# Decay attention, MLP and gated convolution on one core: two sums of each half unit as adding DMAs, a third place for z, and ks by transposes

## The chip, the cores and the metric

The kernel runs on one core of one Trainium2 chip. The metric is the time of one execution on the device in microseconds (us); lower is better. The engines: TensorE (PE, with its weight loads as PEld), VectorE (DVE), ScalarE (ACT), GpSimd (POOL) and SyncE (SP), which starts the DMAs. "Granted clock" is the share of TensorE's full speed that it was given.

## What is computed

Three blocks follow one another, for 4 batches, 8 heads, 768 positions and a head size of 48 (8 x 48 = 384 columns). All data are float32; the weights come as float64 words and are taken apart on the chip.

```python
mag = np.sqrt(a_re * a_re + a_im * a_im)
scale = np.minimum(mag, 0.999) / (mag + 1e-06)
for t in range(S):                      # attention with a complex decay
    S_re, S_im = ar * S_re - ai * S_im + k_t (x) v_t, ar * S_im + ai * S_re
    y[:, :, t] = q_t . S_re
u = x + (x^T @ U @ V)^T                 # mixes all positions of a batch
x = u + relu(u @ w_ch1) @ w_ch2
gate = sigmoid(conv5(x))
out = (gate * (x @ w_val)) @ w_out
```

## The kernel before, in words

`chunked_path` writes the program as a list of operations (class `Program`): each has an engine, an estimated cost, and its dependences. A list scheduler (`lay`, `order`) then sets the order on each engine by urgency plus a bias from the table `URGE`, whose keys are a stage and an engine ("a12S": batch 1, third unit, SP; "m00V": batch 0, first MLP half, DVE; "w3A": weights, fourth group, ACT). On the chip each engine, SP's and POOL's queues among them, runs its operations in that order; only semaphores hold it. `T` makes a tile in a pool; a pool with `bufs` places per tag makes a new tile wait until the oldest one's readers are through.

A batch's attention (`attention`, called by `attend`) runs in three *units* of 256 positions, named by batch and first position (0, 256, 512). The 128 partitions hold 8 heads x 16 groups of 16 positions. Each unit has these stages:

- `z` (pool `p2`, two places) receives `a_re` and `a_im`. In `xa` the decay is normalised, in two halves ("groups"), and `z` becomes the running product over 8 positions (`s1`, `s2`).
- The products are combined across the groups (`qd`, `psT`, `un`, `tot`, `cx`, `psC`), and give the factors `fs`. The result carried to the next unit is `ng`.
- The correction, once for each half, in the loop over `groups`: three products with `fs` put one part into `xc` (as `y2`) and the other into `z`; DVE adds `y2` to `z` (128x768); ACT squares it; DVE adds real and imaginary squares (128x384); ACT takes a logarithm and an exponential; DVE makes `qh` and the scaled `z` with `q` and `k`.
- `z` is stored to a DRAM tile `kd`, and `z` and `qh` are transposed on PE (`pst`) and copied by ACT into `kT` and `qT`.
- For each of the unit's two chunks of 128 positions: `ks`, the same keys with positions on the partitions, is loaded from `kd` (not for the last chunk of a batch); PE makes the scores (`pss`, masked by DVE into `mt`), the state update (`pkv`, added into `st`) and the output (`py`, copied to `yt`). `yt` goes to DRAM (`yd`), and `pxu` collects `xu`, the product with `U`, over the batch.

`moe(b)` then works in two halves of 384 positions: `pu` (with `xuh`, made from `xu`), `m3u`, twelve steps of `ph`, `hp` and `px`, `m3x`, the gate `g`, `pv`, `m3g`, `po`, and the store of `ob`. Each fp32 product is three matmuls of split operands (`mm3`), so DVE and ACT split every operand. `moe(0)` needs the `xu` of all three units of batch 0. Attention of batch b+1 is spread among the matmuls of `moe(b)`. `load_weights` loads 30 raw tiles of 384 KB and converts each: a shift and two merges on DVE (`wt`), two checks and a copy on ACT (`ab`, `w`), a subtraction on DVE (`w`). `w1s` and `w2s` serve `ph` and `px`, `wvs` and `wos` serve `pv` and `po`. The conversions are free to stand anywhere in the order; they run among batch 0's attention.

In the rows all tensor operations have the line of a helper: L551 `tt` (DVE), L567 `stt`, L579 `tsc`, L589 `act`, L600 and L612 matmuls, L621 `transpose`, L631 `dma`. So an operation is named by its tiles.

Of the kernel before, what the change touches and what calls it, by code (L numbers as in the profile page):

```python
# [499 lines left out]
def chunked_path(ctx, tc, outer, q, k, v, a_re, a_im, moe_U, moe_V, w1, w2, w_val, conv_w, w_out, out):  # L500
# [219 lines left out]
    def load_weights():  # L720
# [7 lines left out]
        raw = []  # L728
        for i, (_, _, src, kk, c) in enumerate(todo):
            st = T("wts", [128, PW, 2], I32, f"w{i}", f"raw{i}")  # L730
            sv = src.bitcast(I32).rearrange("(k p) f -> k p f", p=128)[kk]
            dma(st.rearrange("p n w -> p (n w)"), sv[:, 2 * PW * c : 2 * PW * (c + 1)])
            raw.append(st)
        for i, (to, key, *_) in enumerate(todo):
            g.kind = f"w{i // 6}"
            x = T("p3", [128, PW], F32, "g", f"wt{i}")
            single(x, raw[i])
            to[key] = T("wts", [128, 2, PW], F32R, f"w{i}", f"w{i}")
            act(to[key][:, 0], x)
            sub("V", to[key][:, 1], x, f32(to[key][:, 0]))  # L740
# [12 lines left out]
    def attention(b, u0, R):  # L753
# [129 lines left out]
        kd = T("dram", [128, R * 2 * D], F32, "kd", "kd" + n)  # L883
        kdw = kd.rearrange("(h k) f -> k h f", k=16)
# [3 lines left out]
        dma(qk[:, 0], rows(q))  # L888
        dma(qk[:, 1], rows(k))
        qk = qk.rearrange("p c (j d) -> p c j d", d=D)  # L890
        x = T("p1", [128, 16 * 3 * D], F32, "xc", "xc" + n)[:, : R * 3 * D].rearrange("p (j c d) -> p j c d", c=3, d=D)
# [310 lines left out]
```

## Time and profile before

| | us |
|---|---|
| Median of 3 runs (lowest, highest) | 761.53 (759.87, 761.7) |
| The profiled execution's own time | 758.62 |
| Its span | 756.9 |
| PE busy | 620.4 (82%) |
| PEld busy | 567.6 (75%) |
| DVE busy | 622.6 (82%) |
| ACT busy | 445.0 (59%) |
| POOL busy | 2.7 (0%) |
| DMA queue of SP | 67.86 MB, 33.3% of 16 engines' time |

The shares are means over stages with different limits. In the profile's strip of 40 slices, PE is nearly idle in the first three and near full from the tenth on, and DVE is at 9 tenths from the second slice through most of the program. A row of the profile names an operation as out<-in with its shape; an "idle before" time names what ended the engine's wait. In the chain of waits each piece was released by the one before it. The granted clock is 0.94 on average.

### The profile page before, as it was taken

How to read it: one execution, taken by the hardware profiler on the slowest of the kernel's cores; microseconds unless marked ns; L12 is line 12 of the kernel's file. 1: busy time of each engine (PE TensorE's matmuls, PEld its weight loads, DVE VectorE, ACT ScalarE, POOL GpSimd, SP SyncE). 2: the span in 40 equal slices, each digit the busy share in tenths (PEclk: the TensorE clock that was granted, in tenths of full speed). 3: DMA queues.
4: the chain of work that ended last, by engine and by line, in shares of the span. 5: the costliest groups of instructions: out<-in, count | busy, mean ns of one | idle time of the engine just before them, and what ended most of it. 6: DMA issues, size and time to landing. Idle time of an engine off the chain costs nothing.

```text
span 756.9 us, 12129 instructions
## 1 busy us (share of the span) xinstructions
PE 620.4 (82%) x4314; PEld 567.6 (75%) x4314; DVE 622.6 (82%) x1545; ACT 445.0 (59%) x1100; POOL 2.7 (0%) x31
## 2 busy tenths in 40 slices
PE   0003927768997999989999899999999999999994
PEld 0002816556996999869988799889899998899984
DVE  5999999999989989999599899897898875516261
ACT  7899935656458654774478437843774545414253
POOL 1000000000000000000000000000000000000000
PEclk9999558697999999999999999999999999999997
DMA  6984506460052640540515503413142231100000
GB/s 130 320 310 123 128 21 157 120 159 26 1 146 64 162 108 4 147 105 2 144 45 160 133 1 103 108 43 104 43 127 74 64 94 42 43 1 1 1 32 36
DMA packets 80740, 68.71 MB, mean 91 GB/s; under 512 B 52000, under 2 KB 67360, under 8 KB 80672
## 3 DMA queue, kind: packets, MB, share of 16 engines
q1 hardware_dynamic: 80672, 67.86, 33.3%
q8 instruction: 36, 0.59, 0.3%
q14 instruction: 32, 0.26, 0.1%
HBM read 48.97 MB, written 18.87 MB: 90 GB/s over the span
## 4 chain that ended last, share of the span: by engine, by line
PE 53%; DVE 25%; ACT 10%; DMA 8%; issue 2%; SPq 1%; ACTq 0%; DVEq 0%
PE ph L600 17%; PE px L600 16%; DVE z L551 4%; DVE xc L551 4%; PE pss L600 3%; PE py L612 3%; PE pv L600 3%; PE po L600 3%; ACT xa L589 3%; DVE g L567 3%; DMA z<-in_a_im_dram 3%; DMA kd<-z 2%; DVE s L551 2%; PE pkv L612 2%; DMA ks<-kd 2%
## 5 line engine op out<-in xcount | busy, mean ns | idle before, releaser
L600 PE MATMUL ph<-m3u,w 128*128 128x384 f32 x864 | 209.8, 351 | 3.0 <-ACT m3u L589 2.5
L600 PE MATMUL px<-hp,w 128*128 128x384 f32 x864 | 206.2, 345 | 0.4 <-DVE xt L551 0.4
L600 PEld LDWEIGHTS ph<-m3u,w 128*128 128x128 f32 x864 | 156.4, 193 | 9.2 <-ACT m3u L589 4.1
L600 PEld LDWEIGHTS px<-hp,w 128*128 128x128 f32 x864 | 152.4, 188 | 3.7 <-issue 1.9
L589 ACT ACTIVATE hp<-ph 128x384 fp32r<-128x384 f32 x96 | 46.7, 489 | 105.3 <-PE ph L600 97.3
L567 DVE SCALAR_TENSOR_TENSOR hp<-ph,hp 128x384 fp32r<-128x384 f32 x96 | 52.8, 553 | 59.0 <-ACT hp L589 58.7
L600 PE MATMUL pss<-qT,kT 96*128 96x128 f32 x384 | 56.5, 291 | 6.5 <-ACT qT L589 6.5
L600 PEld LDWEIGHTS pss<-qT,kT 96*128 96x128 f32 x384 | 52.2, 203 | 9.4 <-ACT qT L589 8.0
L551 DVE TENSOR_TENSOR s<-xa,z 128x192 f32<-128x192 f32 x168 | 54.6, 351 | 0.8 <-ACT z L589 0.2
L567 DVE SCALAR_TENSOR_TENSOR g<-xt,cw,g 128x384 f32<-128x384 f32 x96 | 53.0, 609 | 0.0
L600 PE MATMUL pv<-m3x,w 128*128 128x384 f32 x216 | 47.0, 358 | 4.8 <-DVE m3x L551 3.9
L621 PE MATMUL pst<-eye_r,xc 128*96 128x128 f32 x192 | 32.7, 292 | 21.2 <-ACT xc L589 18.6
L600 PE MATMUL po<-w,m3g 128*128 128x384 f32 x216 | 47.2, 352 | 3.2 <-ACT m3g L589 2.2
L621 PE MATMUL psT<-eye_r,qd 128*96 128x128 f32 x24 | 5.8, 325 | 47.0 <-ACT qd L589 47.0
L600 PEld LDWEIGHTS pv<-m3x,w 128*128 128x128 f32 x216 | 38.3, 195 | 7.5 <-DVE m3x L551 5.2
L589 ACT ACTIVATE xa<-xa,cb 128x384 f32<-128x384 f32 x72 | 41.8, 610 | 3.5 <-DVE xa L567 2.0
L600 PEld LDWEIGHTS po<-w,m3g 128*128 128x128 f32 x216 | 36.5, 188 | 8.3 <-ACT m3g L589 2.9
L621 PEld LDWEIGHTS pst<-eye_r,xc 128*96 128x96 f32 x192 | 23.7, 135 | 24.4 <-ACT xc L589 18.8
L612 PEld LDWEIGHTS pkv<-vt,ks 128*96 128x96 f32 x320 | 32.4, 178 | 9.3 <-DMA ks<-kd 3.7
L612 PE MATMUL py<-mt,vt 128*64 128x128 f32 x384 | 39.0, 292 | 0.1
L621 PEld LDWEIGHTS psT<-eye_r,qd 128*96 128x96 f32 x24 | 3.0, 147 | 47.9 <-ACT qd L589 47.5
L612 PE MATMUL pkv<-vt,ks 128*96 128x48 f32 x320 | 32.9, 260 | 7.1 <-DMA ks<-kd 7.1
(150 smaller groups left out, 1162.9 us busy)
## 6 DMA issues: line engine op xcount, KB each, us to landing
raw<-in_moe_w_ch_dram SPq DMA_DIRECT2D x24, 384.0 KB, 8.0
kd<-z SPq DMA_DIRECT2D x24, 384.0 KB, 3.8
ks<-kd SPq DMA_DIRECT2D x20, 384.0 KB, 4.2
z<-in_a_re_dram SPq DMA_DIRECT2D x12, 384.0 KB, 4.7
z<-in_a_im_dram SPq DMA_DIRECT2D x12, 384.0 KB, 5.6
qk<-in_k_dram SPq DMA_DIRECT2D x12, 384.0 KB, 4.2
qk<-in_q_dram SPq DMA_DIRECT2D x12, 384.0 KB, 5.2
vt<-in_v_dram SPq DMA_DIRECT2D x24, 192.0 KB, 3.0
```

The costliest lines, as they stand in the source:

```text
L551: e, cost, lambda: engines[e].tensor_tensor(out=real(o), in0=real(a), in1=real(b), op=op), views(a, b), [o]
L567: lambda: nc.vector.scalar_tensor_tensor(out=real(o), in0=real(a), scalar=real(s), in1=real(b), op0=o0, op1=o1),
L589: return nc.scalar.activation(real(o), real(a), func, scale=real(scale), **kw)
L600: "P", cost, lambda: nc.tensor.matmul(real(o), real(lhsT), real(rhs), start=start, stop=stop),
L612: r = nc.tensor.matmul(ro[idx], real(lhsT), real(rhs), start=start, stop=stop)
L621: op = g.add("P", cost, lambda: nc.tensor.transpose(real(o), real(a), real(idn)), views(a, idn), [o])
```

## The change

Five things are changed:

- In batches 1 to 3 the two sums of each half (`z` plus `y2`, and the two squares) are DMAs issued by POOL that add into their target in SBUF (`dma_add`, called by `more`). In batch 0 both stay on DVE.
- In batch 0 the second unit's `z` has a place of its own, `wo2`, beside the two of `p2`. After it the place holds the raw tiles 28 and 29 (of `w_out`) together, and then their split; both are converted after the second of them.
- In batch 0 no `kd` is written. `ks` is made on PE by four transposes of `kT` at a time (`psk`), copied by ACT.
- `xc` is laid out so that `y2` and the squares lie contiguously.
- The scheduler's costs for some DMAs and all of `URGE` are other numbers, so the whole order is another.

```diff
     def dma(o, a, slow=1.0):
...
-        cost = max(475.0, time)
+        cost = max(475.0, x.shape[0] * x.free / 80.0)
...
+    def dma_add(o, x):
+        time = x.shape[0] * x.free / 67.5
+        return g.add(
+            "G", 560.0, lambda: nc.gpsimd.dma_start(real(o), real(x), accum_op=ALU.add), views(o, x), [o], lat=1500.0 + 1.6 * time
+        )
...
+    BY_DMA = (1,2,3,)
...
+        two = T("wts", [128, 2, PW, 2], I32, "wo2", "raw_wo2")
...
-            st = T("wts", [128, PW, 2], I32, f"w{i}", f"raw{i}")
+            st = two[:, i - 28] if 28 <= i < 30 else T("wts", [128, PW, 2], I32, f"w{i}", f"raw{i}")
...
+        def more(o, x):
+
+            if b in BY_DMA:
+                dma_add(o, x)
+            else:
+                add("V", o, o, x)
...
-        z = T("p2", [128, 16 * 2 * D], F32, "z", "z" + n)[:, : R * 2 * D]
+        z_at = ("wts", "wo2") if b == 0 and u0 == UT else ("p2", "z")
+        z = T(z_at[0], [128, 16 * 2 * D], F32, z_at[1], "z" + n)[:, : R * 2 * D]
...
-            add("V", z, z, y2)
-            act(y2, z, AF.Square)
-            add("V", x2, x0, x1)
-            act(x0, x2, AF.Ln, bias=cb[:, 6:7])
+            more(z.rearrange("p j c d -> p (j c d)"), y2)
+            act(sq, z, AF.Square)
+            nn = sq[:, :, 0]
+            more(y2[:, : nj * D], y2[:, nj * D :])
+            act(x0, nn, AF.Ln, bias=cb[:, 6:7])
...
-            dma(kdw[:, :, j0 * P2 : j1 * P2], z.rearrange("p j c d -> p (j c d)"))
+            if b:
+                dma(kdw[:, :, j0 * P2 : j1 * P2], z.rearrange("p j c d -> p (j c d)"), 2.2)
...
-                dma(ks, kdv[c * kr : (c + 1) * kr].rearrange("k j h e -> (k j) h e"), 1.4)
+                if b:
+                    dma(ks, kdv[c * kr : (c + 1) * kr].rearrange("k j h e -> (k j) h e"), 1.4)
+                else:
+                    for h0 in range(0, H, 4):
+                        psk = T(many[0], [C, 4, P2], F32, many[1], "psk" + nc_)
+                        for i in range(4):
+                            transpose(psk[:, i], kTv[:, h0 + i, cs], ident[:P2, :P2])
+                        act(ks[:, h0 : h0 + 4], psk)
```

Where the order moves, first on DVE just before the first MLP half of batch 0. In the names, a number behind a tile's name is the unit's first position or a buffer; `xa_256` here is batch 1's second unit. Before:

```order
L579 TENSOR_SCALAR wt_1603<-raw_598 128x384
L567 SCALAR_TENSOR_TENSOR wt_1590<-raw_701,wt_1590 128x384
L551 TENSOR_TENSOR xu_993<-xu_993,pxu_512_1584 128x96
L551 TENSOR_TENSOR w_1566<-wt_1452,w_1566 128x384
L567 SCALAR_TENSOR_TENSOR wt_1603<-raw_598,wt_1603 128x384
L579 TENSOR_SCALAR wt_1618<-raw_772 128x384
L567 SCALAR_TENSOR_TENSOR wt_1590<-raw_701,wt_1590 128x384
L551 TENSOR_TENSOR xa_256_1576<-xa_256_1576 128x8x48 x2
L551 TENSOR_TENSOR xl_1639<-xu_993,xh_1627 128x96
L567 SCALAR_TENSOR_TENSOR xa_256_1576<-xa_256_1576 128x8x48
L579 TENSOR_SCALAR xuh_1629<-xl_1639 32x96 x8
```

Of the change, up to the same `xuh`:

```order
L553 TENSOR_TENSOR w_1610<-wt_1491,w_1610 128x384
L569 SCALAR_TENSOR_TENSOR xa_256_1531<-xa_256_1531 128x8x48 x2
L553 TENSOR_TENSOR xa_256_1531<-z_256_1447,xa_256_1531 128x8x96
L553 TENSOR_TENSOR xu_1165<-xu_1165,pxu_512_1631 128x96
L553 TENSOR_TENSOR xa_256_1531<-z_256_1447,xa_256_1531 128x8x96
L553 TENSOR_TENSOR xl_1660<-xu_1165,xh_1655 128x96
L553 TENSOR_TENSOR s_1_0_1663<-un_0_1617 96x128
L581 TENSOR_SCALAR xuh_1657<-xl_1660 32x96 x8
```

All thirty tiles' shifts stand ahead of `xuh` before, and 24 of the change; between the last `xu` and `xuh` no weight is left, and batch 1's second unit is further on.

PE, at the third unit of batch 0, first chunk. Before, where `ks` is loaded by a DMA:

```order
L621 MATMUL pst_512_1422<-eye_r,xc_512_1251 96x128 x4
L600 MATMUL pss_512_0_1439<-qT_512_1354,kT_512_1375 128x128 x4
L600 MATMUL pss_512_0_1450<-qT_512_1354,kT_512_1375 128x128 x4
L612 MATMUL py_512_0_1464<-qT_512_1354,st_128 64x128 x2
...
L600 MATMUL pss_512_1_1492<-qT_512_1354,kT_512_1375 128x128 x3
L612 MATMUL pkv_512_0_1501<-vt_122,ks_512_0_1454 96x48 x8
```

Of the change:

```order
L623 MATMUL pst_512_1455<-eye_r,xc_512_1353 96x128 x4
L623 MATMUL psk_512_0_1465<-eye_r,kT_512_1410 128x96 x4
L623 MATMUL psk_512_0_1475<-eye_r,kT_512_1410 128x96 x4
L602 MATMUL pss_512_0_1488<-qT_512_1396,kT_512_1410 128x128 x4
L602 MATMUL pss_512_0_1498<-qT_512_1396,kT_512_1410 128x128 x4
L614 MATMUL pkv_512_0_1505<-vt_122,ks_512_0_1478 96x48 x8
```

`pkv` has moved from behind the chunk's `py` and the next chunk's first scores to right behind its own scores, and its `ks` comes from two groups of transposes.

ACT in the first unit of batch 1, where the adds begin (`xc_0` is that unit's, its squares read the `z_0` that a DMA has added to, and the rows with `cb` are the logarithms behind the second add). Of the change:

```order
L591 ACTIVATE xc_0_1875<-z_0_816 128x8x2x48
L591 ACTIVATE tot_256_1980<-ng_0_1858 96x2x8
L591 ACTIVATE w_1982<-wt_1791 128x384
L591 ACTIVATE hp_0_1993<-ph_0_1925 128x384
L591 ACTIVATE xc_0_1875<-z_0_816 128x8x2x48
L591 ACTIVATE hp_0_2020<-ph_0_1954 128x384
L591 ACTIVATE un_256_1961<-un_256_1961 96x96 x2
L591 ACTIVATE xc_0_1875<-xc_0_1875,cb 128x384
L591 ACTIVATE xc_0_1875<-xc_0_1875 128x384
L591 ACTIVATE w_2047<-wt_1977 128x384
L591 ACTIVATE hp_0_2057<-ph_0_2015 128x384
L591 ACTIVATE xc_0_1875<-xc_0_1875,cb 128x384
```

The `hp` copies that free `ph` for PE stand between the squares and logarithms that wait for the adds.

## Rows read from the trace of the kernel before

**Rows 1.** Busy time by stretch: us, length, busy (x instructions) by engine, clock, DMA.
```profile
0.00:176.50 176.50, 73.32 (x537) 58.74 (x537) 165.99 (x442) 131.85 (x372) 2.34 (x28) 0.82 0.58 160
176.50:745.00 568.50, 545.44 (x3768) 507.63 (x3769) 456.51 (x1103) 309.50 (x714) 0.33 (x3) 0.99 0.27 70
745.00:756.90 11.90, 1.67 (x11) 1.27 (x9) 0.14 (x1) 3.66 (x16) 0.00 (x0) 0.73 0.16 56
```

**Rows 2.** PE's timeline at the first ph: start us, us, operation, idle before.
```profile
176.55 1.80 PE L600 MATMUL ph<-m3u,w 128*128 128x384 f32 x4 [0.81 <-ACT m3u L589]
```

**Rows 3.** Waits of PE, 176 to 757 us: us in total, times, longest us.
```profile
PE pv L600 <- DVE m3x L551: 3.9, 4, 1.6
...
PE pkv L612 <- DMA ks<-kd: 3.1, 3, 2.4
PE ph L600 <- ACT m3u L589: 2.5, 4, 0.8
```

**Rows 4.** Busy time in two passages between MLP halves, columns as in group 1.
```profile
230.00:250.00 20.00, 15.64 (x129) 13.22 (x128) 19.94 (x39) 16.64 (x34) 0.11 (x1) 1.00 0.21 53
330.00:350.00 20.00, 16.73 (x84) 13.84 (x81) 19.67 (x64) 10.17 (x34) 0.00 (x0) 0.91 0.23 66
```

**Rows 5.** Chain of waits, 149 to 162 us: start us, us, what.
```profile
149.59 0.88 DVE z L551
...
150.49 5.03 DMA kd<-z
...
155.53 3.93 DMA ks<-kd
...
159.50 1.56 PE pkv L612 x16
```

**Rows 6.** Timeline of ACT and PE, 145 to 154 us, third unit of batch 0.
```profile
147.19 0.49 ACT L589 ACTIVATE xo<-pxt 128x384 f32<-128x384 f32 x1 [1.71 <-PE pxt L621]
...
150.56 1.05 PE L621 MATMUL pst<-eye_r,z 128*96 128x128 f32 x8 [0.20 <-ACT qT L589]
...
152.49 0.59 ACT L589 ACTIVATE kT<-pst 96x512 f32<-96x512 f32 x1
```

**Rows 7.** Timeline of DVE, 81 to 89 us.
```profile
82.40 0.55 DVE L567 SCALAR_TENSOR_TENSOR wt<-raw,wt 128x384 int32<-128x384 int32 x1
...
83.77 1.02 DVE L551 TENSOR_TENSOR xa<-xa 128x384 f32<-128x384 f32 x2
```

**Rows 8.** Groups of DVE by form: count, busy us, mean ns, idle before.
```profile
L551 DVE TENSOR_TENSOR mt<-pss,cmask 128x512 f32<-128x512 f32 x48 | 32.4, 683 | 2.1 <-PE pss L600 1.8
...
L551 DVE TENSOR_TENSOR xc<-xc 128x384 f32<-128x384 f32 x48 | 26.0, 549 | 0.1
...
L551 DVE TENSOR_TENSOR z<-z,xc 128x768 f32<-128x768 f32 x24 | 22.6, 949 | 0.1
...
L579 DVE TENSOR_SCALAR wt<-raw 128x384 int32<-128x384 int32 x30 | 10.4, 352 | 0.0
```

**Rows 9.** DMA issues: operation, count, KB each, median us to landing.
```profile
kd<-z SPq DMA_DIRECT2D x24, 384.0 KB, 3.8
...
z<-in_a_re_dram SPq DMA_DIRECT2D x12, 384.0 KB, 4.7
z<-in_a_im_dram SPq DMA_DIRECT2D x12, 384.0 KB, 5.6
...
xt<-yd SPq DMA_DIRECT2D x24, 192.0 KB, 2.6
out_dram<-ob SPq DMA_DIRECT2D x24, 192.0 KB, 1.9
```

**Rows 10.** Groups of ACT by form: square, logarithm, exponential of the correction.
```profile
L589 ACT ACTIVATE xc<-z 128x768 f32<-128x768 f32 x24 | 20.2, 843 | 10.4 <-DVE z L551 10.2
...
L589 ACT ACTIVATE xc<-xc,cb 128x384 f32<-128x384 f32 x24 | 14.5, 611 | 7.7 <-DVE xc L551 7.7
...
L589 ACT ACTIVATE xc<-xc 128x384 f32<-128x384 f32 x24 | 12.2, 518 | 0.4
```

More of the change, by code (lines that the diff above doesn't have):

```diff
@@ L737, in load_weights @@
             single(x, raw[i])
-            to[key] = T("wts", [128, 2, PW], F32R, f"w{i}", f"w{i}")
-            act(to[key][:, 0], x)
-            sub("V", to[key][:, 1], x, f32(to[key][:, 0]))
+            done = [(i, to, key, x)]
+            if i == 28:
+                late = done
+                continue
+            if i == 29:
+                two = T("wts", [128, 2, 2, PW], F32R, "wo2", "wo2")
+                done = late + done
+            for j, to, key, x in done:
+                to[key] = two[:, j - 28] if i == 29 else T("wts", [128, 2, PW], F32R, f"w{j}", f"w{j}")
+                act(to[key][:, 0], x)
+                sub("V", to[key][:, 1], x, f32(to[key][:, 0]))
     xts, xus, yds, state, carry = {}, {}, {}, {}, {}
@@ L770, in attention @@
         a3 = T("p1", [128, 16 * 3 * D], F32, "xa", "xa" + n)[:, : R * 3 * D].rearrange("p (j c d) -> p j c d", c=3, d=D)
-        z = T("p2", [128, 16 * 2 * D], F32, "z", "z" + n)[:, : R * 2 * D]
-        dma(z[:, : R * D], rows(a_re))
-        dma(z[:, R * D :], rows(a_im))
+        z_at = ("wts", "wo2") if b == 0 and u0 == UT else ("p2", "z")
+        z = T(z_at[0], [128, 16 * 2 * D], F32, z_at[1], "z" + n)[:, : R * 2 * D]
+        dma(z[:, : R * D], rows(a_re), 1.6)
+        dma(z[:, R * D :], rows(a_im), 1.6)
         ab = z.rearrange("p (c j d) -> p j c d", c=2, d=D)
@@ L881, in attention @@
             act(fs_[:, 1, 0], fs_[:, 1, 2], scale=-1.0)
-        kd = T("dram", [128, R * 2 * D], F32, "kd", "kd" + n)
-        kdw = kd.rearrange("(h k) f -> k h f", k=16)
+        if b:
+            kd = T("dram", [128, R * 2 * D], F32, "kd", "kd" + n)
+            kdw = kd.rearrange("(h k) f -> k h f", k=16)
+            kdv = kd.rearrange("(h k) (j e) -> k j h e", k=16, j=R)
         qT = T("p1", [P2, 128 * 16], F32, "qT", "qT" + n)[:, : 128 * R].rearrange("p (h k j) -> p h k j", h=H, j=R)
@@ L887, in attention @@
         qk = T("p1", [128, 2, 16 * D], F32, "qk", "qk" + n)[:, :, : R * D]
-        dma(qk[:, 0], rows(q))
-        dma(qk[:, 1], rows(k))
+        dma(qk[:, 0], rows(q), 1.5)
+        dma(qk[:, 1], rows(k), 1.5)
         qk = qk.rearrange("p c (j d) -> p c j d", d=D)
-        x = T("p1", [128, 16 * 3 * D], F32, "xc", "xc" + n)[:, : R * 3 * D].rearrange("p (j c d) -> p j c d", c=3, d=D)
-        x0, x1, x2 = x[:, :, 0, :], x[:, :, 1, :], x[:, :, 2, :]
-        y2 = x[:, :, 0:2, :]
+        x = T("p1", [128, 16 * 3 * D], F32, "xc", "xc" + n)
         zr, xr = z, x
@@ L896, in attention @@
             b0, b1, nj = j0 // RB, j1 // RB, j1 - j0
-            z, x, zb = zr[:, j0:j1], xr[:, j0:j1], zv[:, b0:b1]
-            x0, x1, x2 = x[:, :, 0, :], x[:, :, 1, :], x[:, :, 2, :]
-            y2 = x[:, :, 0:2, :]
+            z, x, zb = zr[:, j0:j1], xr[:, j0 * 3 * D : j1 * 3 * D], zv[:, b0:b1]
+            y2, x0 = x[:, : 2 * nj * D], x[:, 2 * nj * D :].rearrange("p (j d) -> p j d", d=D)
+            sq = y2.rearrange("p (c j d) -> p j c d", c=2, d=D)
+            qh = y2.rearrange("p (j c d) -> p j c d", c=2, d=D)
             ms = [128, nj, 2, D]
@@ L902, in attention @@
             bs = [128, b1 - b0, RB, 2, D]
-            yv = y2.rearrange("p (b j) c d -> p b j c d", b=b1 - b0)
+            yv = qh.rearrange("p (b j) c d -> p b j c d", b=b1 - b0)
             mul("V", yv, fs_[:, b0:b1, 0:2].unsqueeze(2).to_broadcast(bs), zb[:, :, :, 1:2, :].to_broadcast(bs))
@@ L906, in attention @@
             mul("V", zb[:, :, :, 0, :], fs_[:, b0:b1, 1:2].to_broadcast(hf), zb[:, :, :, 0, :])
-            add("V", z, z, y2)
-            act(y2, z, AF.Square)
-            add("V", x2, x0, x1)
-            act(x0, x2, AF.Ln, bias=cb[:, 6:7])
+            more(z.rearrange("p j c d -> p (j c d)"), y2)
[3 more added lines that the diff above has]
+            act(x0, nn, AF.Ln, bias=cb[:, 6:7])
             act(x0, x0, AF.Exp, scale=-1.0)
-            mul("V", x2, x2, x0)
+            mul("V", nn, nn, x0)
             mul("V", x0, qk[:, 1, j0:j1], x0)
-            stt(x0, x2, 2.0, x0, ALU.subtract, ALU.mult)
-            qh = x[:, :, 1:3, :]
+            stt(x0, nn, 2.0, x0, ALU.subtract, ALU.mult)
             mul("V", qh, qk[:, 0, j0:j1].unsqueeze(2).to_broadcast(ms), z)
             mul("V", z, x0.unsqueeze(2).to_broadcast(ms), z)
-            dma(kdw[:, :, j0 * P2 : j1 * P2], z.rearrange("p j c d -> p (j c d)"))
+            if b:
+                dma(kdw[:, :, j0 * P2 : j1 * P2], z.rearrange("p j c d -> p (j c d)"), 2.2)
             for src, dst in ((z, kT), (qh, qT)):
@@ L926, in attention @@
                     act(to, pst.rearrange("p j (k h) -> p k h j", h=H))
-        kdv = kd.rearrange("(h k) (j e) -> k j h e", k=16, j=R)
         qTv = qT.rearrange("p h k j -> p h (k j)")
@@ L942, in attention @@
                 kr = C // R
-                dma(ks, kdv[c * kr : (c + 1) * kr].rearrange("k j h e -> (k j) h e"), 1.4)
+                if b:
+                    dma(ks, kdv[c * kr : (c + 1) * kr].rearrange("k j h e -> (k j) h e"), 1.4)
[5 more added lines that the diff above has]
+                        act(ks[:, h0 : h0 + 4], psk)
             st = state.get(b)
```

34 rows, old and new, of the table URGE are left out of this document.

## The prediction

> **What bounds the kernel now.** I read three stretches first [rows 1]. Up to 176.5 us TensorE (PE) works 73.3 us and VectorE (DVE) 166.0. From 176.5 to 745 us PE works 545.4 of 568.5, DVE 456.5. The last 12 us are the last store and the flag. The border is the first `ph` of batch 0, at 176.55 us [rows 2]: the MLP of a batch needs `xu` of its whole sequence, so all of batch 0's attention lies before it. The kernel is thus DVE's queue and batch 0's chain up to 176.5, and PE's own work after it. After the border only 568.5 - 545.4 = 23.1 us are open, in small waits of PE, for `m3x`, `m3u` and `ks` among others [rows 3], bunched where one half of the MLP ends and the next begins: in 230 to 250 us PE works 15.6 of 20 and DVE 19.9, in 330 to 350 PE 16.7 and DVE 19.7 [rows 4]. So time comes off in three ways: an earlier first `ph`, shorter passages from half to half, or a stall that PE is spared.
>
> **ks by transposes (batch 0).** Six `kd` stores and five `ks` loads go. In the chain of batch 0's third unit the last `z` product ends at 150.47 us, `kd` takes 5.03 us, `ks` 3.93, and `pkv` starts at 159.50 [rows 5]. In the new order PE runs the two groups of `psk` right behind the unit's `pst`. Their parts: the eight transposes of `z` behind the last product took 1.05 us and ended at 151.61; the last `kT` copy, two groups behind, ended at 153.08; eight more transposes at 1.05 give 154.13; two copies out of PSUM at 0.49 each (the row of `xo`, the same 128x384) give 155.1 [rows 6]. That is 159.5 - 155.1 = **4.4 us** earlier. PE issues 40 more transposes (5 chunks x 1.05 = 5.3 us) and ScalarE (ACT) 10 more copies (4.9 us), where PE is busy 73 of 176.5 us and ACT 131.9 [rows 1]: besides the two copies on the chain, nothing. Were ACT full there, all 4.9 us would come back.
>
> **DVE's queue before the first `ph`.** By the order, before the first `m3u` subtraction DVE now runs 6 fewer `wt` shifts, 9 fewer `wt` merges and 4 fewer `w` subtractions, but 2 more products of 768 columns, 1 more step of 384 and 2 small ones of batch 1. A step of 384 lasts 0.55 us and two of them 1.02, so neighbours overlap by 0.08 [rows 7]; start to start a shift takes 0.35 - 0.08 = 0.27 us, a step of 384 takes 0.47, one of 768 takes 0.87 [rows 8]. So 6 x 0.27 + 13 x 0.47 = 7.7 us less and 2 x 0.87 + 0.47 + 0.3 = 2.5 more: 5.2 us less. The third place for `z` makes this possible: the `xa` and `z` work of units 256 and 512 moves forward, before and among unit 0's corrections, and fills DVE in place of weights. Queue (5.2) and chain (4.4) must both shrink; I take the smaller, **-4.4 us**, which needs both parts. The weights left out come later, among the first half's `ph`; PE needs `wvs` and `wos` only at its end, so I cost that at nothing. The two raw tiles that wait for the third `z` serve `po`, the half's last step: nothing, unless DVE fills up there.
>
> **Adds by DMA (batches 1 to 3).** DVE loses 18 sums of 768 columns and 18 of 384 (3 batches x 3 units x 2 halves; [rows 8] count 24 of the first kind with batch 0's): 18 x (0.87 + 0.47) = 24.1 us of the 456.5. DVE is not what PE waits for most of that time, so only the passages count. From the first `m3x` of a half to the next half's first `hp`, six times, DVE has 332 rows before and 343 in the new order; each at its shape's mean less the overlap of 0.08, they take 140.2 us and 137.1: 14 fewer steps of 384, 2 fewer of 768 and 4 fewer masks (0.68 each) of attention, but 8 more 384-wide steps of weights and MLP, 6 more of 192 and some small ones. The first passage alone goes from 28.2 to 24.6. With DVE at 19.9 and 19.7 of 20 there, I take all of it: **-3.1 us**.
>
> What an adding DMA takes, no row shows: GpSimd has issued none. Bounds: moving 384 KB once is the `kd` row, 3.8 us, and 192 KB the store row, 1.9 [rows 9]; twice the bytes, since the target is read too, 7.6 and 3.8. So a half's two adds last 5.7 to 11.4 us. I take 4.7 and 2.6, the rows of the `z` and `xt` loads, as `kd` is nearest in bytes and path: 7.3. Between them and behind them stand ACT's square, logarithm and exponential, 0.84 + 0.61 + 0.52 = 1.97 us [rows 10]. The cover: from the last product before the first add to the first product behind the second one DVE has other rows for 8.9 to 11.1 us in ten halves, 13.5 to 19.6 in six and 5 in the last unit's two. 7.3 + 2.0 = 9.3 fits the ten's mean of 9.7, so I cost the adds at nothing; that cover is thin. Behind a square that waits on ACT stands the next `hp` copy, as the order shows, and PE waits for that.
>
> The second load of a pair of `z` lands 0.9 us after the first, 5.6 against 4.7 [rows 9]: two transfers in flight delay one another. The new order issues the halves' adds in pairs. The Trainium skill ("DMA: Bandwidth & Descriptors", section Issuing engines are not separate DMA queues) says that DMAs started by different engines share the same 16 DMA engines; by that, GpSimd's own queue spares the adds nothing. The same page's fit for a DMA from GpSimd (section Anatomy of one DMA) would give 2.0 + 0.9 = 2.9 us for the long add, an estimate from that page which no row here shows, and with it the sum would stay as it is.
>
> **Sum.** The profiled execution took 758.62 us with a span of 756.9. 758.6 - 4.4 - 3.1 = 751.1. The median of the three runs, 761.53, lies 2.9 above that execution, so I give 761.5 - 7.5 = **754.0**. A change within 0.3%, 2.3 us, can't be told from none here.
>
> **Rivals.** (a) *More of PE's 23.1 us goes.* For it: DVE's load after the border falls from 80% to 76%, and the whole order is drawn up anew. If the queue's 5.2 us count and a third of the 23.1, it is -13: 748.5. Against: the passages also wait on ACT, whose work doesn't shrink.
> (b) *Slower: the adds land late.* At the upper ends, 11.4 + 2.0 = 13.4 us against 9.7 of cover is 3.7 us in ten halves, 37 us of waiting on DVE and on ACT, with `hp` copies queued behind the squares. If PE passes on half of it, +18.5 - 7.5 = +11: 772.5. It decides from where a half's two adds together pass 7.7 us, which is close to my 7.3. Against: DVE has 112 us of idle time there, and an order in which `hp` is not next in line loses less.
> (c) *No change.* The first adds, in the first half's `ph`, meet DVE with the weights that were put off. If the 7.7 us of these run into the first passage, they give back the gain at the start: 761.5 - 7.5 + 7.7 = 761.7.
> (d) *The third place does nothing.* Unit 512's early work is done sooner, but the queue stays full, and the chain is as long. Then the transposes alone remain, and the queue's 5.2 goes to waits: 758.4, with the passages' 3.1.
>
> **Chances.** Forecast 0.45, (a) 0.18, (b) 0.22, (c) 0.11, (d) 0.04. The range goes from 744, which is (a) with half of the 23.1 us in place of a third (761.5 - 5.2 - 11.6 = 744.7), to (b)'s 772; what lies beyond, adds that land later still among it, is left out. Forecast, (a) and (d), 0.67, are faster, less 0.02 for a gain within 2.3 us: 0.65; (c) and these 0.02 are no change, 0.13; (b) is slower, 0.22. The forecast's own range is 750 to 758.
>
> **What would show it.** The first `ph` at 172 us, `pkv` of unit 512 with no `DMA ks` ahead of it, DVE 24 us less busy. From the first `ph` to PE's last `po` 565 us instead of 568, with some 545 of PE work. The adds' rows: landing under 5 and 3 us, no waits of `xc` squares for DMA over 1 us in sum per half. I am wrong if the first `ph` stays at 176, if ACT shows long waits for `z` or `xc` from GpSimd's queue and PE shows waits for `hp`, or if the idle time after the border grows.

## The result, and the profile after

The change is slower: 771.24 us (769.04 to 772.06, four runs) against 760.71 (759.87 to 761.7) for the kernel before on the same chip, a ratio of 1.0131 with a 95% interval of 1.0104 to 1.0159. The ratio is taken over all runs and so differs a little from the quotient of the medians. Forecast were 754.0 us, and the whole of what is wrong lies behind the border, the first `ph`.

The profiled execution took 772.06 us with a span of 770.3, 13.4 more than before. (The medians lie 10.5 apart: before's profiled execution, 758.62 us, was shorter than its median, and the change's longer.) Busy time by stretch, up to the first `ph` and from it to PE's last `po`, first of the change and then of the kernel before for the same two borders (its own last `po` starts at 746.1); columns as in [rows 1]:

```profile
0.00:173.10 173.10, 64.82 (x577) 54.44 (x577) 160.87 (x428) 133.40 (x382) 2.33 (x28) 0.93 0.50 138
173.10:759.70 586.60, 556.53 (x3775) 520.53 (x3775) 439.84 (x1081) 309.18 (x714) 31.54 (x39) 0.96 0.37 86
```
```profile
176.60:746.10 569.50, 546.49 (x3774) 508.68 (x3775) 456.41 (x1103) 309.90 (x714) 0.33 (x3) 0.99 0.27 70
```

The start got 3.5 us shorter. DVE has the work less that was to go: 439.8 us against 456.4 in the second stretch. And that stretch is 586.6 - 569.5 = 17.1 us longer. Two things make it up. PE stands idle for 586.6 - 556.5 = 30.1 us where it was 23.0: 7.1. And PE is *busy* 10.0 us longer with the same matmuls (3775 records against 3774), while its mean granted clock fell from 0.99 to 0.96.

The first `ph` [rows 2], PE's waits from there on [rows 3], and the DMAs [rows 9]:

```profile
173.11 5.37 PE L602 MATMUL ph<-m3u,w 128*128 128x384 f32 x15 [0.99 <-ACT m3u L591]
```
```profile
PE pkv L614 <- DMA ks<-kd: 4.4, 4, 3.0
PE pv L602 <- DVE m3x L553: 4.4, 4, 1.5
PE ph L602 <- ACT m3u L591: 3.8, 5, 1.5
PE pxt L623 <- ACT yt L591: 2.8, 2, 2.1
PE py L614 <- DVE mt L553: 2.5, 2, 1.5
```
```profile
z<-xc POOLq DMA_DIRECT2D x18, 384.0 KB, 4.4
kd<-z SPq DMA_DIRECT2D x18, 384.0 KB, 4.3
...
xc<-xc POOLq DMA_DIRECT2D x18, 192.0 KB, 3.5
```

The adds land in 4.4 and 3.5 us, close to the 4.7 and 2.6 taken for them. Still ACT waits for them, 19.5 us in all (list of ACT's waits, 173 to 760 us: total, times, longest):

```profile
ACT xc L591 <- DMA z<-xc: 11.5, 10, 2.6
...
ACT xc L591 <- DMA xc<-xc: 8.0, 6, 2.5
```

Where the clock fell is seen in five stretches of 12 us around waits of PE (columns as above, the granted clock third from the end). None of them was at full clock; by (1 - 0.72) x 2 x 12 = 6.7 us each, and 3.4 in the last, PE ran at 1.2 instead of 2.4 GHz for some 30 us in these five alone:

```profile
229.00:241.00 12.00, 10.94 (x79) 9.98 (x79) 5.58 (x12) 9.58 (x18) 0.98 (x2) 0.72 0.34 56
336.00:348.00 12.00, 9.52 (x34) 8.45 (x35) 10.90 (x32) 7.36 (x20) 2.37 (x3) 0.72 0.62 137
400.00:412.00 12.00, 10.93 (x53) 10.44 (x54) 12.00 (x32) 9.83 (x23) 0.11 (x1) 0.72 0.24 54
434.00:446.00 12.00, 10.21 (x85) 9.31 (x85) 6.94 (x14) 7.04 (x18) 0.86 (x1) 0.72 0.67 145
488.00:500.00 12.00, 11.10 (x71) 10.39 (x73) 10.68 (x22) 6.51 (x11) 0.00 (x0) 0.86 0.04 11
```

In the second of these stretches, PE's timeline has two short waits, and behind them 18 `ph` matmuls that take 6.26 us, 348 ns each, where matmuls of this size run at about half of that at full clock (below):

```profile
336.92 1.34 PE L602 MATMUL pu<-vst,xuh 128*128 128x384 f32 x3 [1.71 <-DVE xuh L581]
339.74 6.26 PE L602 MATMUL ph<-m3u,w 128*128 128x384 f32 x18 [1.49 <-ACT m3u L591]
```

The first of the five stretches follows a late add. In the chain of waits, 218 to 229 us, a `z` add takes 7.61 us to land; the square, `yt` and PE's scores stand in line behind it:

```profile
220.39 7.61 DMA z<-xc
...
228.77 0.59 ACT yt L591
...
229.40 1.79 PE pss L602 x8
```

### The profile page after: what moved, and what is told of

It is laid out like the page before. It is cut to its first block, busy times and chain, and to the rows that moved or that the text cites. A ratio compares the mean times of both kernels' runs of the same rounds, so it can differ in the third digit from the quotient of the medians.

```text
span 770.3 us, 12314 instructions
## 1 busy us (share of the span) xinstructions
PE 621.9 (81%) x4354; PEld 575.1 (75%) x4354; DVE 600.9 (78%) x1509; ACT 445.7 (58%) x1110; POOL 33.9 (4%) x67
## 4 chain that ended last, share of the span: by engine, by line
PE 52%; DVE 17%; DMA 14%; issue 7%; ACT 7%; SPq 2%; POOL 0%; POOLq 0%; ACTq 0%; DVEq 0%
PE ph L602 15%; PE px L602 15%; PE pv L602 4%; DMA raw<-in_moe_w_ch_dram 4%; PE pst L623 4%; PE pss L602 3%; DMA z<-xc 3%; PE py L614 3%; DVE g L569 3%; DMA ks<-kd 2%; DVE xc L553 2%; PE pkv L614 2%; PE po L602 2%; DVE z L553 2%; DVE s L553 2%
## 5 line engine op out<-in xcount | busy, mean ns | idle before, releaser
L602 PE MATMUL ph<-m3u,w 128*128 128x384 f32 x864 | 213.6, 355 | 4.1 <-ACT m3u L591 3.8
L602 PE MATMUL px<-hp,w 128*128 128x384 f32 x864 | 203.8, 344 | 1.8 <-ACT hp L591 1.4
L602 PEld LDWEIGHTS ph<-m3u,w 128*128 128x128 f32 x864 | 158.1, 196 | 10.8 <-ACT m3u L591 6.2
L602 PE MATMUL pv<-m3x,w 128*128 128x384 f32 x216 | 50.5, 379 | 5.2 <-DVE m3x L553 4.4
L602 PEld LDWEIGHTS pv<-m3x,w 128*128 128x128 f32 x216 | 41.6, 211 | 7.9 <-DVE m3x L553 5.7
L623 PEld LDWEIGHTS pst<-eye_r,xc 128*96 128x96 f32 x192 | 23.6, 136 | 23.7 <-issue 12.8
L553 DVE TENSOR_TENSOR mt<-pss,cmask 128x512 f32<-128x512 f32 x48 | 32.6, 683 | 8.8 <-PE pss L602 8.6
L553 DVE TENSOR_TENSOR xa<-xa 128x384 f32<-128x384 f32 x48 | 25.9, 550 | 16.1 <-ACT xa L591 16.0
L591 ACT ACTIVATE kT<-pst 96x512 f32<-96x512 f32 x48 | 26.9, 589 | 19.3 <-PE pst L623 19.0
L623 PE MATMUL pst<-eye_r,z 128*96 128x128 f32 x192 | 31.3, 301 | 5.3 <-DVE z L553 4.3
```

What stands on the lines that cost most here:

```text
L553: e, cost, lambda: engines[e].tensor_tensor(out=real(o), in0=real(a), in1=real(b), op=op), views(a, b), [o]
L591: return nc.scalar.activation(real(o), real(a), func, scale=real(scale), **kw)
L602: "P", cost, lambda: nc.tensor.matmul(real(o), real(lhsT), real(rhs), start=start, stop=stop),
L623: op = g.add("P", cost, lambda: nc.tensor.transpose(real(o), real(a), real(idn)), views(a, idn), [o])
```

## The experiments

Two theories. **L**: the adds land late, ACT and PE wait, and the clock halves (half clock: 1.2 in place of 2.4 GHz). **O**: the order that was drawn up anew is worse behind the border, whoever adds. Two more points came up on the way: whether half clock is brought about by PE's standing still, and whether the earlier start is a gain or a *loan*, paid back behind the border.

All runs in one table. "ph" is the start of the first `ph` and "ph to po" the time to the start of PE's last `po`, both in the profiled execution, with PE's busy and idle time between. The time is the median of the runs; the ratio is to the kernel before on the same chip, with its 95% interval.

| run | ph | ph to po | PE busy | idle | us | ratio |
|---|---|---|---|---|---|---|
| before | 176.6 | 569.5 | 546.5 | 23.0 | 760.7 | |
| the change | 173.1 | 586.6 | 556.5 | 30.1 | 771.2 | 1.0131 (1.0104 to 1.0159) |
| e1 | 171.4 | 585.0 | 554.3 | 30.7 | 769.4 | 1.0110 (1.0034 to 1.0186) |
| e2 | 169.0 | 588.5 | 557.4 | 31.1 | 775.1 | 1.0177 (1.0131 to 1.0222) |
| e3 | 172.4 | 607.8 | 563.1 | 44.7 | 792.8 | 1.0393 (1.0348 to 1.0438) |
| e4 | 168.8 | 597.2 | 562.2 | 35.0 | 777.5 | 1.0188 (1.0142 to 1.0234) |
| e5 | 181.6 | 570.0 | 548.2 | 21.9 | 765.9 | 1.0064 (1.0036 to 1.0092) |
| e6 | 176.7 | 588.1 | 552.9 | 35.2 | 777.8 | 1.0209 (1.0169 to 1.0248) |
| e7 | 188.7 | 593.2 | 554.8 | 38.4 | 789.7 | 1.0352 (1.0311 to 1.0392) |
| e8 | 182.7 | 592.7 | 555.8 | 36.9 | 787.3 | 1.0329 (1.0286 to 1.0373) |
| e9 | 184.8 | 568.9 | 548.0 | 20.9 | 768.6 | 1.0095 (1.0058 to 1.0132) |
| e10 | 183.3 | 573.0 | 549.7 | 23.3 | 769.3 | 1.0099 (1.0062 to 1.0137) |
| e11 | 177.0 | 584.7 | 556.9 | 27.8 | 768.4 | 1.0096 (1.0060 to 1.0131) |
| e12 | 176.7 | 576.5 | 554.5 | 22.0 | 766.7 | 1.0077 (1.0043 to 1.0111) |
| e13 | 173.0 | 577.9 | 553.9 | 24.0 | 762.4 | 1.0014 (0.9983 to 1.0044) |
| e14 | 167.9 | 587.4 | 549.4 | 38.0 | 767.7 | 1.0084 (1.0052 to 1.0116) |
| e15 | 182.7 | 567.5 | 545.3 | 22.2 | 762.9 | 1.0025 (0.9992 to 1.0058) |
| e16 | 177.5 | 567.5 | 547.6 | 19.9 | 763.5 | 1.0041 (1.0012 to 1.0071) |
| e17 | 168.6 | 578.6 | 553.9 | 24.7 | 759.5 | 0.9971 (0.9943 to 0.9999) |
| e18 | 168.3 | 576.9 | 554.7 | 22.2 | 758.0 | 0.9953 (0.9928 to 0.9979) |

### e1 to e4: adds back on DVE, and the order drawn up with either table

e1 issues every instruction of the change in its order, but the 36 adds run on DVE, each at the place at which its DMA was planned. e2 plans anew without adds by DMA; e3 and e4 are the change and e2 with the table `URGE` of before.

```diff
 e1, in dma_add:
-            "G", 560.0, lambda: nc.gpsimd.dma_start(real(o), real(x), accum_op=ALU.add), views(o, x), [o], lat=1500.0 + 1.6 * time
+            "G", 560.0, lambda: nc.vector.tensor_tensor(out=real(o), in0=real(o), in1=real(x), op=ALU.add), views(o, x), [o], lat=1500.0 + 1.6 * time
 e2 and e4:
-    BY_DMA = (1,2,3,)
+    BY_DMA = ()
 e3 and e4: URGE as before
```

> The changed kernel with its order kept to the instruction on PE, ACT and SP: the 36 sums of batches 1 to 3 are planned as the adding DMAs, at the same places, but issued as DVE additions (0.95 and 0.55 us each, 24 us more on DVE). Theory L (the adds land late, ACT waits for them with PE's work queued behind, PE idles and its clock halves): ACT's 19.5 us of waits for adds go, PE's idle time from the first ph to the last po falls from 30 us to 23 or less, half-clock stretches after 190 us from 38 us to under 15, and the time is 755 to 762. Theory O (the new order has worse passages between MLP halves, whoever adds): 768 to 775, with the same dips of the clock at the same places.

> The changed kernel with the sums back on DVE in all batches, its URGE table kept, and the order drawn up anew by the scheduler for that. Theory L: 755 to 760, the first ph near 173 us and PE's idle time after it near the 23 us of before. Theory O: the table was made for other costs, so 765 to 780. A redraw moves the time in itself, so a result between says that both weigh.

> The whole change (adds by DMA, third place, ks by transposes, new costs) with the URGE table of the kernel before. Theory L: the adds cost about as much under any table, so 10 us or more above e4. Theory O: within 4 us of e4.

> The third place of z, ks by transposes and the new costs, with the sums on DVE and the URGE table of the kernel before. Theory L: 755 to 760, since the batch 0 parts bring the first ph to 173 us and nothing else is lost. Theory O: the order is drawn up anew here too and can lose as much: 762 to 775. The pair e3, e4 shows the price of the adds under one table, as the changed kernel and e2 do under the other.

With DVE adding again in e1, 461.4 us busy in place of 439.8, the stretch behind the border is 585.0 us:

```profile
171.40:756.40 585.00, 554.34 (x3775) 513.51 (x3775) 461.43 (x1117) 307.79 (x714) 0.32 (x3) 0.97 0.26 68
```

So in the change's own order adds by DMA are 586.6 - 585.0 = 1.6 us dearer than adds on DVE, and without any late add this order is still 15.5 us longer than before's (585.0 against 569.5). The 1.6 us are a net. PE's instructions are the same in both, in the same order, so their starts can be compared, two of the change and the same two of e1:

```profile
274.83 1.53 PE L614 MATMUL pkv<-vt,ks 128*96 128x48 f32 x16 [0.89 <-DMA ks<-kd]
398.38 0.66 PE L623 MATMUL pxt<-eye_r,yt 128*128 128x128 f32 x4 [2.13 <-ACT yt L591]
```
```profile
270.66 1.53 PE L614 MATMUL pkv<-vt,ks 128*96 128x48 f32 x16 [0.62 <-DMA ks<-kd]
399.62 1.11 PE L623 MATMUL pxt<-eye_r,yt 128*128 128x128 f32 x4 [2.28 <-ACT yt L591]
```

At the first `ph` e1 is 1.7 us ahead, behind the change's late `z` add 4.2, at 400 us 1.2 *behind*, at the last `po` 3.3 ahead. So e1 wins where the change's late add stood and loses elsewhere, with 21.6 us more of work on DVE in an order that was not drawn up for it. Its 769.4 us are what O had expected, but how much of the 15.5 is the order alone and how much these sums, e1 can't tell. e2 and e4 are drawn up for adds on DVE, with the new table and the old one, and are no shorter: 588.5 and 597.2 us. Between e4 and e3, under the old table, the adds cost 10.6 us (15.3 between the medians, the start included), as L had expected. e4's 777.5 us lie above what either theory had given it.

### e5 to e8: before's order kept

The planner first plans the program of before and takes its start times as the priorities of the new one, so that what was there before should keep its place. It does so in part: it still places each operation when its plan has the inputs ready, and by the traces 218 of DVE's 1067 instructions behind the border stand in another order in e6 than before, 220 of 1063 in e8 and 131 of 1085 in e12; in e7, which is planned anew, 547 of 1545 in all. (`xc` is laid out as in the change in all of these, and below.)

```diff
+    old = {op.key: op.start for op in build((), False, False, False)[0].order()}
+    g, fine = build(*flags)
...
-        g.emit()
+        g.emit(old)
...
 e5: flags: ks of batch 0 by transposes
 e6: flags: BY_DMA = (1, 2, 3)
 e8: flags: all parts of the change
 e7: no old order; before's parts and table, DMA costs as in the change
```

> The kernel of before with one part of the change alone: ks of batch 0 by transposes. The order of the work is not planned anew: every instruction that was there before keeps its place, and the new transposes and copies stand where their inputs are ready. If the order after the border is what the change loses by (O), this run keeps before's 570.0 us from the first ph to the last po (568 to 572) and has the first ph at 172 to 174: 755 to 759 us. If the late adds are the cause (L), the same is expected, since no add is a DMA here. If the transposes themselves are dear on PE or ACT before the border, the first ph stays at 176 or later: 761 or more.

> The kernel of before with the other part alone: the two additions of each half unit of batches 1 to 3 are done by DMAs, and every instruction that was there before keeps its place. L: the wait for the adds shows in full, ACT waits some 20 us for z and xc and the run takes 770 to 785 us. O: the adds fit into what DVE leaves between its rows, as the prediction had it, and the run takes 757 to 764 us, with 570 to 575 us from the first ph to the last po.

> The kernel of before, with its table, and only the planner's prices of DMAs as in the change: nothing is computed in another way, the order alone is planned anew. O: a new order by itself costs as much as the change did after the border: 766 to 790 us, with 580 us or more from the first ph to the last po and PE's busy time in it above 550 us. L: nothing lands later than before, so 758 to 764 us.

> All three parts of the change (adds by DMA, third place of z, ks by transposes) with before's order of the work kept. O: the start gain of 3 to 4 us without the loss after the border, 754 to 762 us, that is 10 us or more below the change. L: the adds are late here too, 768 us or more.

Both theories find support. In e6 the adds are late: 588.1 us behind the border, 18.6 more than before, with the same start. ACT waits 25.2 us for them; what of the 18.6 is due to the instructions that were moved is open:

```profile
176.70:764.80 588.10, 552.93 (x3775) 511.37 (x3775) 436.03 (x1067) 309.12 (x714) 31.52 (x39) 0.98 0.36 86
```
```profile
ACT xc L607 <- DMA xc<-xc: 12.9, 9, 3.0
ACT xc L607 <- DMA z<-xc: 12.3, 7, 3.3
```

In e7 nothing is computed in another way; the planner only has other prices for DMAs. It loses 23.7 us behind the border and 12 ahead of it, and PE waits for `m3x` 16.0 us where it was 3.9 [rows 3]:

```profile
PE pv L618 <- DVE m3x L569: 16.0, 4, 6.4
```

So an order that is merely another can cost more than the whole change did. O expected 754 to 762 for e8, and it failed: with all parts, an order near before's has the late adds (23.2 us behind the border). e5 kept its 570.0 us, as expected, but its start was 5 us later and not 4 earlier: unit 512's last `z` product of DVE ran at 155.23 us where before has 149.59 [rows 5], so DVE's queue was late before the transposes could help. Ahead of the border 36 of DVE's 442 instructions stand in another order than before; whether that made it late is not settled.

### e9, e10 and e14: the new start in front of before's order

Up to the first `ph` the priorities are those of e4, from there on before's, shifted. e9 has two places for `z`, e10 three. Work that before does ahead of the border and e4 doesn't is put in among the start's (e9, e10), or right behind the border (e14).

```diff
+    first, then = plan((), True, True, True), plan((), False, False, False)
+    old = {k: t - border[1] + border[0] for k, (t, _) in then.items()}
+    old.update({k: t for k, (t, _) in first.items() if t < border[0] or k not in old})
```

> No add by DMA, z at its two places, ks of batch 0 by transposes. Up to the first ph the instructions stand as in the run of the batch 0 parts under the old table (first ph at 168.8 there, with the third place), from it on as in the kernel before. If the loss of the change comes from the order behind the border (O), the time from the first ph to the last po stays at 570 (568 to 573) and the whole is before's with an earlier start: first ph 169 to 173, 753 to 758 us. If an earlier start is by itself paid back later (units that then find their inputs late), the time from ph to po grows by 3 us or more and the run takes 759 to 762.

> The same with the third place of z as well, so all that the change does in batch 0. First ph 168 to 171; O with the third place of use: 752 to 756 us; if the third place does nothing: as the run without it; if an earlier start is paid back later: 759 or more.

> As the run with the new start and the third place, but what before did ahead of the first ph and the new start does not is put behind the border instead of among the start's work: up to the first ph the instructions are those of the run of the batch 0 parts under the old table (first ph 168.8), from it on before's order. First ph 168 to 171. O: 568 to 573 us from there to the last po and 750 to 756 us in all, below both kernels. If the 9 us of DVE work that is now behind the border is paid for there, 577 or more from ph to po and 760 to 766 us.

e9 keeps before's time behind the border and e10 nearly so (568.9 and 573.0), which is O's point, but they lose the start (184.8 and 183.3). e14 shows why. Its first `ph` is at 167.95 us, and then PE stands for 13.9 us, because DVE does what the start had left out before it gets to the second `m3u`:

```profile
167.95 1.01 PE L618 MATMUL ph<-m3u,w 128*128 128x384 f32 x2 [0.93 <-ACT m3u L607]
182.86 3.57 PE L618 MATMUL ph<-m3u,w 128*128 128x384 f32 x10 [13.91 <-DVE m3u L569]
```

### e11 and e12: one of the two adds alone

e6 with only the first (`z`) or only the second add (`xc`) by a DMA.

```diff
 e11:
-            more(y2[:, : nj * D], y2[:, nj * D :])
+            add("V", y2[:, : nj * D], y2[:, : nj * D], y2[:, nj * D :])
```

> The kernel of before with its order, and only the first of the two additions (z, 384 KB each, 18 of them) by a DMA. With both it lost 18.6 us between the first ph and the last po. If each add pays for its landing after the fact (L as a chain, z then square then xc then ln), z with 4.0 of 7.2 us of landing takes 9 to 12 us of it: 769 to 773. If one add alone fits into the cover of the half unit (landing 4.4 and less, cover 9.7 in the mean), it is 760 to 764.

> The same with only the second addition (xc, 192 KB each, 18 of them) by a DMA. Chain: 6 to 9 us of loss, 766 to 770. Cover: 759 to 763.

No cover holds even one of them: 15.2 us behind the border for `z` (in a profiled execution of 774.2 us, above the median of its nine) and 7.0 for `xc`. The medians, 768.4 and 766.7, are what L as a chain had expected, or just under it. In e12 none of the 7.0 is idle time of PE, which is 22.0 us where before has 23.0; PE is busy 8.0 us longer. So a loss can be paid wholly in clock. In both runs the same holds of the order as in e6.

### e13: the change, with PE kept busy in six waits

Ahead of six first matmuls PE runs matmuls into the same PSUM tile that are then overwritten; they wait for nothing that the real ones wait for.

```diff
+    FILL = {"pu_1_0": 8, "ph_1_0": 8, "pv_0_1": 5, "pv_1_0": 6, "pv_1_1": 8, "pkv_2_256_1": 14}
...
+                for _ in range(k):
+                    nc.tensor.matmul(at, w[:, 1, : o.shape[0]], w[:, 0, :], start=True, stop=True)
+                return fn()
```

> The change, with idle matmuls put on PE ahead of six first matmuls that it waits before (pu and ph of the half at 337, pv at 320, 401 and 489, pkv at 436; 49 matmuls of 128x384, each sized to the wait that the change's trace shows). Their results are overwritten; every other instruction stands as in the change. If the half clock that follows is brought about by PE's standing still there (O's second half), the stretches at 339.5, 400.9, 435.1 and 489.7 (23.8 us at 1.2 GHz in all) go, PE's own work gets some 6 us shorter and the run takes 763 to 769 us. If the half clock comes from something else (the load of the other engines or of the DMAs at these places), the stretches stay and the run takes 771 to 776 us, since the idle matmuls only add.

762.4 us, and its ratio of 1.0014 (0.9983 to 1.0044) lies clear of the change's 1.0131 (1.0104 to 1.0159). The five stretches, at the places to which the work has moved:

```profile
229.00:241.00 12.00, 10.74 (x79) 9.75 (x78) 5.99 (x14) 9.81 (x19) 0.50 (x2) 0.72 0.34 65
333.00:345.00 12.00, 10.12 (x49) 8.09 (x49) 11.69 (x35) 7.80 (x22) 2.62 (x3) 1.00 0.66 150
397.00:409.00 12.00, 8.39 (x46) 7.83 (x47) 11.26 (x28) 9.15 (x21) 0.11 (x1) 0.86 0.23 55
429.00:441.00 12.00, 12.00 (x115) 10.81 (x114) 8.21 (x17) 9.67 (x24) 1.82 (x3) 1.00 0.95 204
480.00:492.00 12.00, 11.65 (x82) 11.01 (x83) 12.00 (x26) 8.32 (x14) 0.00 (x0) 1.00 0.26 49
```

The first place was not filled, and there it is 0.72 as before; the others are at 1.00, 0.86, 1.00 and 1.00. DVE, ACT and the DMAs do the same work, so in these four places the half clock comes from PE's standing still. At the second place:

```profile
332.83 1.55 PE L606 MATMUL pu<-w 128*128 128x384 f32 x8
334.71 1.32 PE L617 MATMUL pu<-vst,xuh 128*128 128x384 f32 x3 [0.33 <-DVE xuh L581]
335.87 1.56 PE L606 MATMUL ph<-w 128*128 128x384 f32 x8
...
338.38 3.07 PE L617 MATMUL ph<-m3u,w 128*128 128x384 f32 x16 [0.22 <-DVE m3u L553]
```

The `ph` matmuls take 3.07 us for 16, 192 ns each, where the change had 348. 49 matmuls that compute nothing (1.55/8 us each, 9.5 us) make the kernel 8.7 us shorter from `ph` to `po`. The Trainium skill ("TensorE: Matmul & The Clock Gate", section A second HAM failure mode) describes a kernel in which frequent short idles of PE between groups of matmuls make its clock swing between the two levels. The change's trace agrees in part: here single waits of 1.5 to 3 us, or two close together, stand ahead of a stretch at half clock. Not every such wait brings one: before's longest wait for `ks` [rows 3], 2.44 us up to 420.11, has full clock around it:

```profile
420.11 1.53 PE L612 MATMUL pkv<-vt,ks 128*96 128x48 f32 x16 [2.44 <-DMA ks<-kd]
417.00:429.00 12.00, 9.56 (x101) 8.94 (x101) 9.17 (x31) 2.65 (x6) 0.00 (x0) 1.00 0.51 126
```

### e15 to e18: is there a version below both?

e15 and e16 are the kernel before with such matmuls (e15: `pu_0_0` 9, `pu_1_0` 7, `pu_2_0` 4, `pv_3_1` 4; e16 without the first). e17 is e14 with the weight splitting placed as in e4, among the first half's `hp`, and what else the start left out moved 10 us back. e18 is e17 with `pu_1_0` 8, `ph_1_0` 4, `pu_2_0` 7 and `pv_3_1` 4.

```diff
 e17:
+    old = {k: t if t >= border[0] else max(t + LATE, border[0] + 3000.0 + 1e-3 * t) for k, t in old.items()}
+    old.update({k: t for k, (t, _) in first.items() if t <= border[0] or k not in old or k in first and first[k][1][0] == 'w'})
```

> The kernel before with idle matmuls on PE ahead of pu of the first, third and fifth half (9, 7 and 4) and of pv of the last (4), where its trace shows waits with half clock behind them. If standing still brings the half clock, before's 13.6 us at 1.2 GHz between 176 and 745 get down to 4 or less and the run takes 755 to 760 us; else 760.5 to 764.

> As the run of before with four places filled, without the one ahead of the first half (there the nine idle matmuls ran at half clock and took 2.88 us of the way to the first ph): pu of the third and fifth half (7 and 4), pv of the last (4). With the half clock brought about by PE's standing still: 566.5 to 568.5 us from the first ph to the last po where before has 569.5, and with a first ph as in before's runs 757 to 760 us, 1 to 3 below before on this chip. If it is of no use there: 569 to 571 and the same time as before.

> No add by DMA, z's third place, ks by transposes. In the run with the new start's exact order DVE did the splitting of ten weight tiles between the first and the second m3u, and PE stood for 13.9 us; here these stand where the run of the batch 0 parts has them (among the first half's hp rows), and all else behind the border as in before. If the earlier start is a gain of its own: first ph 168 to 172, no wait over 5 us behind it, 568 to 575 us to the last po, 750 to 758 us. If what the start leaves out has to be paid for behind the border in any order (a loan, not a gain): 576 us or more, 759 to 768 us.

> The same with idle matmuls ahead of pu and ph of the third half (8 and 4), pu of the fifth (7) and pv of the last (4). If half clock follows PE's standing still: 2 to 6 us less from the first ph to the last po than the run without, and the same first ph.

In e15 and e16 the stretch from `ph` to `po` is 567.5 us, 2.0 less than before, but the times, 762.9 and 763.5, are not below before's and not the 755 to 760 that were expected. e15 lost it at the start, where the added `pu` matmuls took 2.88 us for nine on the chain, with `ks` at 4.54 us and `pkv` at 2.40 ahead of them, where before has 3.93 and 1.56 [rows 5]:

```profile
157.23 4.54 DMA ks<-kd
161.82 2.40 PE pkv L626 x16
...
178.12 2.88 PE pu L603 x9
```

e16's profiled execution is its shortest of twelve (757.9 us, median 763.5), so its profile doesn't tell why the others are longer: open.

e17 answers the question of the loan:

```profile
0.00:168.60 168.60, 69.58 (x579) 55.28 (x579) 156.55 (x430) 132.15 (x379) 2.33 (x28) 0.87 0.51 142
168.60:747.20 578.60, 553.92 (x3773) 516.85 (x3774) 463.96 (x1115) 310.74 (x717) 0.32 (x3) 0.97 0.26 69
```

The first `ph` is 8.0 us earlier than before, and from there to the last `po` it takes 9.1 us more: 156.6 us of DVE's work lie ahead of the border where before has 166.0 [rows 1], and 464.0 behind it where before has 456.4. The first half alone, up to its last `po`, takes 5.5 of the 9.1 (77.7 us from the first `ph` against 72.2), where the weights are split that the start left out. That is what was expected of a loan, though part of the order behind the border is another as well. e17 is 759.5 us and e18 758.0, its ratio 0.9953 (0.9928 to 0.9979). e18 beats both kernels, by 0.5% against before (0.3% between the medians), without any add by DMA; it is 1.7 us shorter than e17 behind the border where 2 to 6 were expected, and its interval overlaps e17's, so what its idle matmuls add to it is not shown.

## Why the prediction was wrong

- *The start, -4.4 us.* Right in size: -3.5, with the first `ph` at 173.1 (forecast 172) and no `ks` DMA ahead of unit 512's `pkv`. (The three traces with this order ahead of the border, the change, e1 and e13, have 171.4 to 173.1, and five with before's, e6, e11, e12 and e16 among them, 176.6 to 177.5.) But it was written as a gain, with the weights left out costed "at nothing". Of the weights' splits (`w<-wt,w`) 23 stand ahead of the first `m3u` in the change and 27 before; DVE's busy time up to the border fell by 166.0 - 160.9 = 5.1 us. In e17 8.0 us of a start won in this way come back as 9.1; rival (c) had that mechanism. In the change itself the first half is only 0.8 us longer than before's (73.0 us from the first `ph` to its last `po` against 72.2), so there the loan is not seen.
- *The passages, -3.1 us.* **This step failed.** DVE's rows in six passages were counted and their difference taken as time. The rows did shrink, from 140.7 to 137.4 us in the traces, each row less the overlap of 0.08 (140.2 to 137.1 forecast). But the passages themselves, from DVE's first `m3x` of a half to its next `hp`, add up to 162.3 us before (28.4, 33.2, 23.9, 28.1, 18.4 and 30.3) and 169.8 in the change (32.9, 30.7, 24.6, 27.9, 25.2 and 28.5): 7.5 more. The first, which was to go from 28.2 to 24.6, went from 28.4 to 32.9, with DVE busy for 25.1 of it, before and then the change:

```profile
226.90:255.30 28.40, 23.62 (x183) 20.69 (x182) 28.33 (x53) 23.21 (x47) 0.11 (x1) 1.00 0.30 77
```
```profile
221.50:254.40 32.90, 27.68 (x190) 24.88 (x186) 25.08 (x51) 23.51 (x54) 1.84 (x3) 0.84 0.46 98
```

  The late `z` add lies in it, and with the adds on DVE (e1) this passage takes 26.9. The fifth went from 18.4 to 25.2, and 25.5 in e1: there the order itself shows, with 55 rows of DVE where before had 36. Nor was DVE full in every passage before: in the sixth its rows fill 18.9 of 30.3 us. A shorter queue of rows says nothing on what each wait ends on; the prediction priced rows, not waits.
- *PE's work as a constant.* The forecast held "some 545 of PE work" fixed and treated only the 23.1 us of idle time as open. **This failed too**: PE's busy time rose by 10.0 us, more than its idle time (7.1). e13 shows the cause: half clock behind short waits. The clock rows of before ([rows 4]: 0.91 at 330 to 350 us) had the sign of it.
- *The adds, at nothing.* Their landing was well guessed (4.4 and 3.5 us against 4.7 and 2.6, sum 7.9 against 7.3), and 7.9 is past the 7.7 from which rival (b) was to decide. They were not free: ACT waited for 16 of the 36, 19.5 us in the change and 25.2 in e6. A cover of 9.7 us in the mean against 9.3 needed leaves many of the cases late, and a wait counts only on that side. What they cost in the change is known only as a net: 1.6 us more than the same sums on DVE. In an order near before's it was 18.6. How the change's 17.1 us divide between late adds and the order stays open; that orders drawn up anew lose 19 to 28 us with no add by a DMA at all is shown (e2, e4, e7), and why they do is not.
- *Rival (b)*, 772.5 us, has the time, 771.2, and in e6 its mechanism. That its +18.5 is met there (18.6) is luck in part, since e6's order moved too, and in the change the share of the late adds is open.

## What to carry to other kernels

Where a long in-order program was tuned by its order, a change that redraws the order has to be priced as a new order: run the old order with the new operations (e6) and the new order with the old operations (e1). Each tells a part, and neither is clean: in e6 the planner moved a fifth of DVE's instructions, in e1 DVE got sums that the order had no room for. The work in a queue is no measure of the time that the queue takes (the six passages). An earlier milestone is a gain only if nothing was moved behind it (e17). And here PE's short waits were often paid twice, as idle time and as half clock behind it; a few matmuls that compute nothing, put where PE would stand, gave back more than they took in the change (e13), and nothing that shows in the kernel before (e15, e16).

## What the runs showed of the hardware

- Behind waits of PE of 1.5 to 3 us stood stretches at 1.2 GHz (granted clock 0.72 over 12 us at four places of the change), but not behind each (1.00 around before's wait of 2.44 us). In e12 the clock was the whole price: idle time 22.0 us against 23.0, busy time 8.0 us more.
- A DMA that adds in SBUF, issued by GpSimd, took 4.4 us in the median for 384 KB and 3.5 for 192 KB in the change, with one of 384 KB at 7.61 us.
- The same instructions don't reach the border at the same time: e15 has those of before up to its added `pu`, and its `pkv` of unit 512 started 2.3 us later (161.82 against 159.50), behind DMAs that landed later. So a change of 2 us there is not to be read from one profile; the time behind the border was steadier (568.9 to 570.0 us in before, e5 and e9).
